# A listed instruction order for the opening of a fused attention and leaky-ReLU kernel, with separate places for four chunks

## The chip, the cores and the metric

The kernel runs on one core of one Trainium2 chip. A core has engines that run at the same time, each with a queue of its own that it works off strictly in order: TensorE (PE, matrix products, with a separate row PEld for the loading of the stationary operand), VectorE (DVE), ScalarE (ACT), GpSimd (POOL) and SyncE (SP), which here only issues DMA transfers. Engines wait for each other through semaphores. PE writes its results to PSUM; ACT and DVE read them from there; POOL and the DMA engines work on SBUF. The metric is the device time of one execution in microseconds (us), and lower is better.

## What is computed

The first part is a decayed linear attention over blocks of 64 tokens, the second a two-layer product with a leaky ReLU between.

```python
intra = np.einsum('bhic,bhjc->bhij', qb, kb) * Dmask[None]
intra = np.einsum('bhij,bhjd->bhid', intra, vb)
inter = np.einsum('bhid,bhde->bhie', qb * lam_pow[None], kv_state)
out[:, :, sl] = intra + inter
kb_dec = kb * rev_pow[None]
kv_state = lam_block * kv_state + np.einsum('bhsd,bhse->bhde', kb_dec, vb)
...
h = x @ w_in                       # x: 3072 x 512, w_in: 512 x 2048, float64
g = np.maximum(0.01 * h, h)
return (g @ w_out).astype(np.float32)   # w_out: 2048 x 512, float64
```

q, k and v are float32 of shape 4 x 8 x 768 x 64; the weights come as float64, and the output is float32.

## The kernel before

**Tiles.** The 3072 tokens are 24 chunks of 128 (two blocks of 64), six to a batch entry. Four chunks make a group of 512 tokens; there are six groups. w_in is cut into eight parts `p` of 256 columns.

**One chunk c.** SP loads k and q (two DMAs of 128 KB each) and v (one of 256 KB). PE transposes k and q (L406, L407), ACT copies the transposes out of PSUM (L414, L415). POOL or DVE scales k in place (L419), DVE or POOL scales the transposed q (L423). PE forms the scores (`go`, L433) and the state products (`kv`, L439); both go to the PSUM tile `psc`, scores in its lower half and states in its upper. DVE multiplies the scores by the decay (L452) and adds the state products to the running state (L457, L459), which POOL scales (L462). PE then forms the chunk's output in `po` (`own`, L472, and the two `inter` parts, L480), with a small copy of two columns between them (L491). ACT and DVE split the output into three float32r parts xh, xl, xm (L507, L508, L510).

**One weight part p.** A float64 half (512 KB) lands in one of three `raw` buffers. ACT makes three pieces of it (L578, L580, L582), DVE shifts and adds them to a float32 (L584, L585); with both halves done, the part is split into wh (ACT or DVE, L591 or L593), wl (DVE, L596) and wm (DVE, L602).

**up(g, p)** multiplies group g by part p: xh·wh and xl·wl for two blocks of 128 columns, an ACT rescale (L658), xm·wm, and the leaky ReLU on ACT (L661), then a store of 512 KB to DRAM (L664). A product of the full group is four matmuls of 512 columns. All `up` of groups 0 and 1 interleave with chunks 4 to 12; groups 2 to 5 follow. After that, `down` (L688) reads the stored results back and multiplies them by w_out; it fills the second part of the time.

**What sets the order.** Every step is an operation added to `Plan` with an engine (or two to choose from), an estimated length and the names it reads and writes; dependencies follow from the names. `emit` (L83) places operations greedily by estimated start time and rank, with PE operations of one round of a chunk locked together (`chains`), sorts them by that time and issues them: each engine's queue has that order for good. A second pass (L146 to L159) re-estimates times, and where PE would idle over 0.4 us it puts in unused 128 x 128 transposes (`busy`, L263) as long as the bank `b10` is not in use. Eleven such transposes run at the start (L268).

**Places.** Chunk c uses place `c % 2` of k, q, v and their transposes (`of`, L326), so chunk c + 2 can't be loaded before chunk c has been used. Scores and states share the one name `psc`: the DVE reads of either wait for both, and both products of the next chunk wait for all those reads.

**The end.** After `emit`, 32 matmuls whose results nothing uses are issued (L793 to L809): 24 with 512 columns on strips of the array, and 8 with 64 columns, which the trace records as 16.

Of the kernel before, what the change touches and what calls it, by code (L numbers as in the profile page):

```python
# [34 lines left out]


class Plan:

# [6 lines left out]
    def __init__(self):  # L45
        self.ops, self.last, self.rank = [], {}, 0.0
        self.chain, self.chains = None, {}
        self.warm, self.slack, self.more = 0.0, 0.0, {}
        self.first = {"PE": 0.0, "ACT": 0.0, "DVE": 3.4, "POOL": 0.0, "DMA": 0.2}
        self.cold, self.idle, self.spare = 6.0, None, None  # L50

    def begin(self, name):
# [30 lines left out]
    def emit(self):  # L83
        n = len(self.ops)
        follows, heads = {}, {}
        for c in self.chains.values():
            m = [i for i in c if "PE" in self.ops[i][0]]
            for i in c[1:]:
                self.ops[m[0]][2].update(self.ops[i][2] - set(c))
            heads[m[0]] = m[1:]  # L90
            follows.update((i, m[0]) for i in m[1:])
# [21 lines left out]
        done = []  # L113
        while len(done) < n:
            best = None
            for e in free:
                for i in able[e]:
                    if e == "PE" and (i != locked[0] if locked else i in follows):
                        continue
                    t = max(free[e], since(i, e))  # L120
                    if (best is None or (t, self.ops[i][3]) < best[:2]) and good(i, e, t):
                        best = (t, self.ops[i][3], i, e)
            t, _, i, e = best
            ways, fn = self.ops[i][:2]
            if i in heads:
                locked = list(heads[i])
            elif locked and i == locked[0]:
                locked.pop(0)
            for x in ways:
# [8 lines left out]
            for u in users[i]:  # L138
                ends[u].append((free[e] + self.more.get(i, 0.0), e))
                left[u] -= 1  # L140
                if not left[u]:
                    for x in self.ops[u][0]:
                        able[x].add(u)
        self.timeline = sorted(done)

# [3 lines left out]
        for t, _, i, e in self.timeline:  # L149
            ways, fn, deps = self.ops[i][:3]  # L150
            t = max([soon[e]] + [over[d][0] + (0.0 if over[d][1] == e != "DMA" else self.SOON[over[d][1]]) for d in deps])
            if e == "PE":
                if self.spare in self.ops[i][4]:
                    self.idle = None
                if self.idle is not None and t > soon[e] + 0.4:
                    self.idle(int((t - soon[e] - 0.2) / 0.22))
# [6 lines left out]
def kernel(  # L163
# [32 lines left out]
    GOFIRST = 3  # L196
    SUBL, FIRST = 0.75, -8.0

    DV = 10
# [22 lines left out]

    W = [[sb([P, 4 * 2 * P], f"w{x}{p}", F32R) for x in "hlm"] for p in range(NP)]
    X = [[sb([P, KO, T], f"x{x}{i}", F32R) for x in "hlm"] for i in range(2)]
# [22 lines left out]
    kqv = [[x[:, i * H * D:(i + 1) * H * D].rearrange("p (h d) -> p h d", h=H) for i in range(2)] for x in kqv_f]  # L247
    kTs, qTs, qsTs = ([part(HP * C).rearrange("p (y t) -> p y t", y=HP) for _ in range(2)] for _ in range(3))
    sc = part(2 * HP * C2).rearrange("p (x y t) -> p x y t", x=2, y=HP)
    state = [part(HP * D).rearrange("p (y d) -> p y d", y=HP) for _ in range(4)]  # L250
# [56 lines left out]
    add("DVE", 1.95, factors_k, [], ["fk", "sc"])  # L307
    add("DVE", 1.25, factors_q, [], ["fq"])
    ENG = {"ACT": nc.scalar, "DVE": nc.vector, "POOL": nc.gpsimd}
# [16 lines left out]
    def of(c):  # L326
        return c // NCB, c % NCB, c % 2

# [98 lines left out]
    def scores(c):  # L427
# [17 lines left out]
        if c < GOFIRST:  # L445
            add("PE", 0.47, go, [f"kT{i}", f"qT{i}"], ["psc"])
        add("PE", 0.47, kv, [f"k{i}", f"v{i}"], ["psc"])
        if c >= GOFIRST:
            add("PE", 0.47, go, [f"kT{i}", f"qT{i}"], ["psc"])

        def uses():
            add("DVE", 0.69, lambda: nc.vector.tensor_tensor(sc, psc[:, :, lower, :], decay, op=ALU.mult), ["psc", "fk"], ["sc"])  # L452
            for t in range(n_pu):
                j = 2 * c + t
                new = state[j % 4]
                if n == 0 and t == 0:
                    add("DVE", 0.42, lambda new=new: nc.vector.tensor_copy(new, pu[0]), ["psc"], [f"st{j % 4}"])  # L457
                else:
                    add("DVE", 0.42, lambda new=new, t=t: nc.vector.tensor_tensor(new, new, pu[t], op=ALU.add),  # L459
                        ["psc"], [f"st{j % 4}"])  # L460
                if n_pu == 2:
                    add("POOL", 0.7, lambda new=new, j=j: nc.gpsimd.tensor_tensor(state[(j + 1) % 4], new, _bc(lam_c, 2, D), op=ALU.mult),  # L462
                        [f"st{j % 4}", "fq"], [f"st{(j + 1) % 4}"])
# [123 lines left out]
    def parts(p, src, keys):  # L587
        wh, wl, wm = W[p]
        def head(e):
            if e == "ACT":  # L590
                nc.scalar.activation(out=wh, in_=src, func=AF.Copy, bias=0.0, scale=NEAR / S)  # L591
            else:
                nc.vector.tensor_scalar(wh, src, NEAR / S, None, op0=ALU.mult)  # L593

        add(("ACT", "DVE"), (1.05, 0.7), head, keys, [f"wh{p}"])
        add("DVE", 1.25, lambda: nc.vector.scalar_tensor_tensor(wl, wh.bitcast(F32), -S, src, op0=ALU.mult, op1=ALU.add),  # L596
            keys + [f"wh{p}"], [f"wl{p}"])
        difference(p)

    def difference(p):  # L600
        wh, wl, wm = W[p]
        add("DVE", 1.25, lambda: nc.vector.scalar_tensor_tensor(wm, wl.bitcast(F32), 1.0, wh.bitcast(F32), op0=ALU.mult, op1=ALU.subtract),  # L602
            [f"wh{p}", f"wl{p}"], [f"wm{p}"])

    def w_in(p):
        for h in range(2):
            to_float32("wi", p, h, w32[:, h, :], f"w32{h}")
        parts(p, w32f, ["w320", "w321"])

# [153 lines left out]
    for n, x in enumerate(seq):  # L763
# [15 lines left out]
        elif x[0] == "wp":  # L779
            if not freed:  # L780
                add("DVE", 0.0, lambda: None, [], ATT + [f"gr{j}" for j in range(NR)])
                add("ACT", 0.0, lambda: None, [], [f"raw{j}" for j in range(NRAW)] + ["t0", "t1"])
# [5 lines left out]
        else:  # L788
            down(*x[1:])
    plan.emit()  # L790


    a, b = ring[0][0], W[0][0]  # L793
    spare = acc[0] + acc[1]

    def strips(n, times):

        k = P // n
        for _ in range(times):
            for i in range(n):  # L800
                r = slice(i * k, (i + 1) * k)
                nc.tensor.matmul(spare[i], lhsT=a[r, 0:P], rhs=b[r, 0:T], start=True, stop=True, skip_group_check=True)  # L802

    strips(2, 6)
    strips(4, 3)
    f = graw[0]
    for _ in range(4):
        for i in range(2):
            nc.tensor.matmul(spare[2][HALF[i], 0:C2], lhsT=f[:, 0:C2], rhs=f[:, 0:C2], start=True, stop=True, skip_group_check=True)  # L809

# [29 lines left out]
```

## Time and profile before

The time is 611.25 us, the median of three runs (610.77 to 612.51). The profiled execution has a span of 610.29 us from its first to its last instruction.

| what | us |
|---|---|
| median of the runs | 611.25 |
| span of the profiled execution | 610.29 |
| PE busy | 601.9 |
| DVE busy | 313.2 |
| ACT busy | 269.9 |
| POOL busy | 86.6 |
| first product with a weight part (`up(0, 1)`) starts | 30.41 |
| last product of `down` starts to end | 605.17 to 606.28 |
| last unused product ends | 609.39 |

"Busy" counts an engine's instructions and leaves out its waits. PE's matmuls overlap in a pipeline, so that a busy PE may still run below its peak; the start-to-start distance of two matmuls is the better price: 0.227 us for 512 columns in the stream that fills most of the span. A wait is given as the idle time ahead of an instruction with what ended it.

### The profile page before, as it was taken

To read this page: it belongs to the slowest core of one execution; us is meant where nothing else is said; L and a number is where in the kernel's file an instruction comes from. 1 tells how busy PE (TensorE), PEld (TensorE's weight loads), DVE (VectorE), ACT (ScalarE), POOL (GpSimd) and SP (SyncE) were. 2 spreads that over 40 slices of the span, in tenths; PEclk is the share of its full clock that TensorE was granted. 3 is DMA by queue.
4 is the path that set the end of the run, shared out by engine and by line. 5 is a ranking of instruction groups with operands and counts; after the bars stand their busy time and mean duration, and the time that the engine had idled before them with its cause. 6 is when DMAs were issued, how large, how long until landed. Compare 5 with 4: busy or idle time off the path is not lost.

```text
span 610.3 us, 13012 instructions
## 1 busy us (share of the span) xinstructions
PE 601.9 (99%) x5426; PEld 497.6 (82%) x5426; DVE 313.2 (51%) x418; ACT 269.9 (44%) x430; POOL 86.6 (14%) x90
## 2 busy tenths in 40 slices
PE   7799999999999999999999999999999999999999
PEld 5688888888888878888788888888888888888887
DVE  5899764334243426326366755545454544636531
ACT  4678974444455646555577522222222313214111
POOL 2564412114133004104000000000000000000000
PEclk9899999999999999999999999999999999999999
DMA  9999775666889878886686843524333343333201
GB/s 201 236 261 263 215 204 126 175 154 176 192 212 245 212 222 219 212 242 212 233 302 219 278 155 103 173 69 139 137 104 134 111 136 111 132 104 126 82 1 69
DMA packets 147754, 105.18 MB, mean 172 GB/s; under 512 B 123632, under 2 KB 124400, under 8 KB 147696
## 3 DMA queue, kind: packets, MB, share of 16 engines
q1 hardware_dynamic: 147552, 104.36, 58.8%
q8 instruction: 42, 0.69, 0.5%
q14 instruction: 16, 0.13, 0.1%
q10 hardware_dynamic: 144, 0.00, 0.0%
HBM read 68.69 MB, written 35.65 MB: 171 GB/s over the span
## 4 chain that ended last, share of the span: by engine, by line
PE 95%; DMA 2%; ACT 1%; DVE 1%; issue 0%; SPq 0%; ACTq 0%
PE b L640 42%; PE b L700 18%; PE po L700 11%; PE psc L700 11%; PE po L313 4%; PE psc L313 4%; PE pt L700 4%; DMA g<-gs 1%; DMA att<-in_v_dram 1%; PE pt L403 1%; DMA att<-in_q_dram 1%; PE po L403 0%; PE psc L802 0%; ACT att L415 0%; PE b L266 0%
## 5 line engine op out<-in xcount | busy, mean ns | idle before, releaser
L682 ACT ACTIVATE xh<-att 128x1024 fp32r<-128x1024 f32 x48 | 50.8, 1060 | 149.1 <-PE b L700 133.6
L683 DVE SCALAR_TENSOR_TENSOR xl<-att,xh 128x1024 fp32r<-128x1024 f32 x48 | 58.7, 1223 | 97.5 <-ACT xh L682 97.5
L640 PE MATMUL b<-xm,wm 128*128 128x512 f32 (+2 forms) x392 | 104.5, 392 | 0.7 <-ACT b L658 0.7
L640 PE MATMUL b<-xh,wh 128*128 128x512 f32 (+2 forms) x392 | 103.2, 386 | 0.8 <-ACT xh L507 0.8
L640 PE MATMUL b<-xl,wl 128*128 128x512 f32 (+2 forms) x392 | 103.4, 387 | 0.0
L640 PEld LDWEIGHTS b<-xh,wh 128*128 128x128 f32 x392 | 72.9, 188 | 16.0 <-ACT xh L507 0.9
L640 PEld LDWEIGHTS b<-xl,wl 128*128 128x128 f32 x392 | 72.7, 188 | 15.1 <-DVE wl L596 0.3
L640 PEld LDWEIGHTS b<-xm,wm 128*128 128x128 f32 x392 | 71.4, 188 | 16.0 <-ACT b L658 1.1
L658 ACT ACTIVATE b<-b 128x512 f32<-128x512 f32 (+2 forms) x97 | 56.1, 580 | 60.6 <-PE b L640 60.5
L661 ACT ACTIVATE gs<-b 128x512 f32<-128x512 f32 (+2 forms) x97 | 57.0, 592 | 44.2 <-PE b L640 38.3
L700 PE MATMUL b<-wh,xh 128*128 128x512 f32 x192 | 74.7, 389 | 0.0
L700 PE MATMUL b<-wl,xl 128*128 128x512 f32 x192 | 74.7, 389 | 0.0
L685 DVE SCALAR_TENSOR_TENSOR xm<-xl,xh 128x1024 fp32r<-128x1024 f32 x48 | 58.7, 1225 | 4.7
L462 POOL TENSOR_TENSOR att<-att 128x256 f32<-128x256 f32 x40 | 34.4, 861 | 58.7 <-DVE att L459 58.7
L700 PEld LDWEIGHTS b<-wh,xh 128*128 128x128 f32 x192 | 36.1, 188 | 7.5
L700 PEld LDWEIGHTS b<-wl,xl 128*128 128x128 f32 x192 | 36.0, 188 | 7.5
L423 POOL TENSOR_TENSOR att<-att 128x512 f32<-128x512 f32 (+1 forms) x20 | 25.3, 1265 | 95.6 <-PE po L313 34.7
L452 DVE TENSOR_TENSOR att<-psc,att 128x512 f32<-128x512 f32 x24 | 16.5, 689 | 43.1 <-PE psc L313 43.1
L584 DVE TENSOR_SCALAR w<-w 128x512 int32<-128x512 int32 x32 | 19.6, 612 | 36.0 <-ACT w L578 35.9
L700 PE MATMUL psc<-wh,xh 128*128 128x512 f32 x96 | 37.3, 389 | 0.0
L700 PE MATMUL psc<-wl,xl 128*128 128x512 f32 x96 | 37.3, 389 | 0.0
L700 PE MATMUL psc<-wm,xm 128*128 128x512 f32 x96 | 37.3, 389 | 0.0
(79 smaller groups left out, 810.4 us busy)
## 6 DMA issues: line engine op xcount, KB each, us to landing
att<-g SPq DMA_DIRECT2D x48, 512.0 KB, 3.3
g<-gs SPq DMA_DIRECT2D x47, 512.0 KB, 4.0
raw<-in_moe_w_in_dram SPq DMA_DIRECT2D x16, 512.0 KB, 5.5
raw<-in_moe_w_out_dram SPq DMA_DIRECT2D x16, 512.0 KB, 4.8
att<-in_k_dram SPq DMA_DIRECT2D x48, 128.0 KB, 4.3
att<-in_v_dram SPq DMA_DIRECT2D x24, 256.0 KB, 4.5
out_dram<-gs SPq DMA_DIRECT2D x23, 256.0 KB, 2.1
wo<-w SPq DMA_DIRECT2D x8, 512.0 KB, 5.9
```

Source lines behind the costliest of these rows:

```text
L313: nc.tensor.matmul(dst[HALF[cols]], lhsT=lhsT[HALF[rows]], rhs=rhs[HALF[rows]], start=start, stop=True, skip_group_check=True)
L423: add(eng, us, lambda: e.tensor_tensor(o, x, _bc(pow_q, 2, 2)[:, :, m, :], op=ALU.mult), ["fq", dep], [f"qsT{i}"])
L452: add("DVE", 0.69, lambda: nc.vector.tensor_tensor(sc, psc[:, :, lower, :], decay, op=ALU.mult), ["psc", "fk"], ["sc"])
L462: add("POOL", 0.7, lambda new=new, j=j: nc.gpsimd.tensor_tensor(state[(j + 1) % 4], new, _bc(lam_c, 2, D), op=ALU.mult), [f"st{j % 4}", "f ...
L584: add("DVE", 0.42, lambda: nc.vector.tensor_scalar(d, d, 3, None, op0=ALU.logical_shift_left), [], [key])
L640: nc.tensor.matmul(dst, lhsT=w[z][:, kk * 2 * P + f * P:kk * 2 * P + (f + 1) * P], rhs=x[z][:, kk, toks], start=start and kk == 0, stop=kk ...
L658: add("ACT", ns, lambda b=b: nc.scalar.activation(out=b, in_=b, func=AF.Copy, bias=0.0, scale=S + 1.0), [], [kb], rank=-1.5)
L661: add("ACT", ns, lambda b=b, r=r: nc.scalar.activation(out=r, in_=b, func=AF.Prelu, bias=0.0, scale=1.0 / WS, alpha=0.01), [kb], [f"gs{jg} ...
L682: add("ACT", 1.05, lambda: nc.scalar.activation(out=h, in_=graw[j], func=AF.Copy, bias=0.0, scale=NEAR), reads, wr("h"))
L683: add("DVE", 1.25, lambda: nc.vector.scalar_tensor_tensor(l, graw[j], 1.0, h.bitcast(F32), op0=ALU.mult, op1=ALU.subtract), reads + [f"rh{ ...
L685: add("DVE", 1.25, lambda: nc.vector.scalar_tensor_tensor(m, l.bitcast(F32), -S, h.bitcast(F32), op0=ALU.mult, op1=ALU.add), [f"rh{j}", f" ...
L700: nc.tensor.matmul(acc[tb][z // 2][:, cols], lhsT=ring[j][z][:, f * T + tb * P:f * T + (tb + 1) * P], rhs=W[pp][z][:, f * d_model:(f + 1) ...
```

## The change

**A listed order.** `ORDER` lists operations 0 to 710 of the plan, which are all of groups 0 and 1, by number; a letter behind a number names the engine where two are possible (a = ACT, v = DVE, p = POOL), and `f6` asks for six unused transposes before the next PE operation. `emit` places these first, in this order, without ranks and without the locked rounds, and goes on greedily behind them. The automatic filling of PE gaps is off; only the listed fillings remain (6, 5, 4 and 3). The queues open as follows (T = transpose, SC = scores, KV = state products, OWN and I0, I1 = output parts, the digit is the chunk):

```
PE after:  f6 Tk0 Tq0 f5 KV0 Tq1 Tk1 SC0 Tk2 OWN0 I0 SC1 I1 Tq2 KV1 f4 OWN1 SC2 I0 I1 KV2 Tk3 Tq3
           OWN2 I0 SC3 I1 KV3 f3 OWN3 I0 I1 Tq4 up(0,1): h h l l, Tk4, m m, up(0,0): h h l l, Tq5 SC4 KV4 ...
SP after:  q0 k0 q1 v0 k1 k2 q2 v2 v1 raw(1) k3 q3 raw(1) v3 q4 raw(0) raw(0) k4 raw(2) q5 raw(2) v4 ...
SP before: k0 q0 v0 k1 q1 v1 raw(1) q2 k2 raw(1) v2 q3 k3 q4 v3 raw(0) k4 q5 v4 raw(0) k5 q6 v5 ...
```

In the DVE queue, the scaling of k of chunk 0 is gone (now POOL's first operation); the copies L491 of chunks 3, 4, 5 and 7 are on DVE; wh of parts 2, 3, 5 and 6 has moved to ACT, wh of parts 4 and 7 to DVE.

**Places.** Chunks 2, 3, 4 and 5 get places of their own in the memory of weight parts 5, 6, 7 and 4, which are written late; a zero-length operation keeps each part from being written before its chunk is done. Chunks 6 and on use the two old places.

**Names.** `psc` is split into `psS` (scores) and `psK` (states).

**The end.** The unused products behind `emit` are gone.

```diff
+        for i, e in self.listed:
+            e = e or next(iter(self.ops[i][0]))
+            assert i in able[e]
+            put(i, e, max(free[e], since(i, e)))
...
-                if self.spare in self.ops[i][4]:
+                if self.spare in self.ops[i][4] and not self.listed:
                     self.idle = None
-                if self.idle is not None and t > soon[e] + 0.4:
+                if i in self.fill:
+                    self.idle(self.fill[i])
+                elif not self.listed and self.idle is not None and t > soon[e] + 0.4:
...
+    OWN = {2: 5, 3: 6, 4: 7, 5: 4}
...
+    for p in OWN.values():
+        for j, (x, y) in enumerate(zip(kqv, (kTs, qTs, qsTs))):
+            z = W[p][j]
+            x.append(z[:, :H * D].rearrange("p (h d) -> p h d", h=H))
+            y.append(z[:, H * D:].rearrange("p (y t) -> p y t", y=HP))
...
-        return c // NCB, c % NCB, c % 2
+        return c // NCB, c % NCB, c % 2 if c not in OWN else 2 + list(OWN).index(c)
...
-            add("PE", 0.47, go, [f"kT{i}", f"qT{i}"], ["psc"])
-        add("PE", 0.47, kv, [f"k{i}", f"v{i}"], ["psc"])
+            add("PE", 0.47, go, [f"kT{i}", f"qT{i}"], ["psS"])
+        add("PE", 0.47, kv, [f"k{i}", f"v{i}"], ["psK"])
...
-            add("DVE", 0.69, lambda: nc.vector.tensor_tensor(sc, psc[:, :, lower, :], decay, op=ALU.mult), ["psc", "fk"], ["sc"])
+            add("DVE", 0.69, lambda: nc.vector.tensor_tensor(sc, psc[:, :, lower, :], decay, op=ALU.mult), ["psS", "fk"], ["sc"])
...
+        if p in OWN.values():
+            i = 2 + list(OWN.values()).index(p)
+            add("DVE", 0.0, lambda: W[p].__setitem__(slice(3), weights(p)), [],
+                [f"{x}{i}" for x in ("k", "q", "v", "kT", "qT", "qsT")] + [f"w{x}{p}" for x in "hlm"])
...
-    strips(2, 6)
-    strips(4, 3)
-    f = graw[0]
-    for _ in range(4):
-        for i in range(2):
-            nc.tensor.matmul(spare[2][HALF[i], 0:C2], lhsT=f[:, 0:C2], rhs=f[:, 0:C2], start=True, stop=True, skip_group_check=True)
```

## The prediction

> **What bounds the kernel now.** I read the page's busy shares and slices first, then the table by stages, then the rows of PE, DVE and SP around the first 40 us, and last the end of the span.
>
> ```profile
> PE 601.9 (99%) x5426; PEld 497.6 (82%) x5426; DVE 313.2 (51%) x418; ACT 269.9 (44%) x430; POOL 86.6 (14%) x90
> ...
> PE   7799999999999999999999999999999999999999
> ...
> DVE  5899764334243426326366755545454544636531
> ...
> PE 95%; DMA 2%; ACT 1%; DVE 1%; issue 0%; SPq 0%; ACTq 0%
> ```
>
> PE is the bound, but its first two slices (15 us each) are not full, and DVE is fullest in slices 2 to 4. The table by stages has, for each stretch, the busy time of PE, PEld, DVE, ACT and POOL, then the granted clock, the share of the DMA engines and GB/s:
>
> ```profile
> 4.00:15.00 11.00, 9.10 (x208) 6.75 (x209) 7.62 (x24) 5.33 (x10) 2.26 (x3) 1.00 1.13 236
> 15.00:25.00 10.00, 7.51 (x248) 5.72 (x251) 8.51 (x14) 6.96 (x13) 6.83 (x7) 1.00 1.02 244
> 25.00:30.40 5.40, 4.62 (x115) 3.80 (x104) 4.35 (x6) 2.70 (x6) 1.49 (x3) 0.69 0.91 228
> 30.40:38.20 7.80, 7.79 (x96) 6.45 (x97) 7.56 (x11) 5.53 (x10) 4.91 (x4) 1.00 1.01 284
> 38.20:55.60 17.40, 17.40 (x305) 14.55 (x305) 16.34 (x23) 15.42 (x29) 8.36 (x7) 1.00 0.90 251
> 100.00:606.20 506.20, 505.24 (x3863) 417.84 (x3861) 233.40 (x291) 198.98 (x307) 43.80 (x48) 1.00 0.55 163
> ```
>
> From 30.4 us on PE has no gap worth a name. So what this change can win lies before 30.4, and in the end. The timeline shows how the opening is lost:
>
> ```profile
> 24.43 1.57 PE L313 MATMUL psc<-att 64*64 64x64 f32 x64 [1.79 <-DMA att<-in_v_dram]
> ...
> 30.41 2.12 PE L640 MATMUL b<-xh,wh 128*128 128x512 f32 x8 [0.78 <-ACT xh L507]
> ```
>
> The scores of chunk 3 wait for its v, which SP issues at 19.07 and which lands at 24.30. Before 30.41 PE does 10 transposes of a tile at 0.44 (start-to-start at 59.27 and 59.70) and four chunks' scores, states and outputs at 2.03 (51.66 to 53.69): 4.4 + 8.1 = 12.5 us. From the first transpose at 4.04 that leaves 30.41 - 4.04 - 12.5 = **13.9 us lost** to waits, unused transposes and half clock. The clock is at half in one stretch of 3.4 us (25.0 to 28.4; 0.69 in the third row). It costs 0.64 on scores and states (1.57 against 0.93), 0.53 on outputs (1.39 against 0.86) and 0.14 on a transpose, 1.3 us together.
>
> DVE is the second bound. In the opening its rows swell whenever POOL works:
>
> ```profile
> 15.90 1.22 DVE L584 TENSOR_SCALAR w<-w 128x512 int32<-128x512 int32 x1
> ```
>
> **The change, part by part.**
>
> *The end.* The last unused product starts at 608.70 and takes 0.69, to 609.39:
>
> ```profile
> 608.70 0.69 PE L809 MATMUL po<-att 128*64 128x64 f32 x16
> ```
>
> The last output transfer is issued at 607.3 and lands 1.7 later, at 609.0. SP waits for both before it closes, so the removal saves 609.39 - 609.0 = **0.4 us**, and no more, since the transfer is next. If that transfer took 0.4 longer, nothing.
>
> *Places and load order.* SP's first 14 entries wait for no buffer now. Equal bytes should land at the times of before: 256 KB by 4.6, 1.28 MB by 9.4, 3.1 MB by 16.4. v of chunk 3 has 4.2 MB up to itself; the 3.1 MB at 16.4, and then 0.5 us for each 128 KB (its pace from 10.4 to 16.4) give 16.4 + 8 x 0.5 = 20.4, at most 21.4 at the pace that followed. So the wait at 24.43 goes, 3 to 4 us earlier. What is late next is DVE.
>
> *The DVE queue to the first product.* I sum the rows of before in the new order, each without its overlap with the row ahead, up to the first state addition of chunk 3: decay factors 3.15, four score products 2.76, seven state operations 2.31, four scalings of q 2.32, three xl 1.80, two xm 1.29, two shifts 1.90, one sum 0.60: 16.1 us from 3.44. Scaling k of chunk 0 (0.67) is on POOL now, beside its landing, where POOL is idle. To this come DVE's own waits. Before they are 5.8 (1.3, 1.9, 0.2, 0.2, 2.1). In the new order: 0.3 for the first transpose; 1.7 for states 0, since v0 lands at 8.2 and PE takes 0.6; 1.3 for scores 0, which PE does behind the transpose of k1, landed at 9.4; 1.0 for scores 1, behind the output of chunk 0. That is 4.3, so the state addition ends at 3.44 + 16.1 + 4.3 = 23.9. Behind it in the chain: an output part on PE 0.4, the sum at L585 (1.1, running since 23.9) and the small copy 0.15, the last output part 0.45, and on ACT wh of part 1 (1.06, behind that sum) and xh 0.5. **The first product starts at 26.7**, against 30.41. The floor that the DMA alone sets is 20.4 + 0.6 + 0.4 + 0.4 + 0.3 + 0.5 + 0.6 for the small waits = 23.2; I use 24.0 for a best case.
>
> *The next weight part.* PE then has up(0, 1), 6 x 0.907 = 5.44, and one transpose, 0.44: it asks for wh of part 0 at 32.6. DVE's sum up to there is 27.1, with 4.3 and another 0.4 of waits: 35.2. In this sum eight rows are slower than the same row with POOL idle (shifts 1.22, 0.84 and 0.84 against 0.43; sums 1.20 and 1.46 against 0.69; wl 1.64 against 1.22; xm 1.07 against 0.69; wh 1.43 against 0.69): 4.4 us of excess. The new order puts two of POOL's scalings into the first 12 us, where DVE waits anyway; without all the excess the 35.2 would be 30.8, under PE's own 32.6. Between 32.6 and 35.2 I take 33.4, nearer to the lower end because of those two. Before, this product started at 38.24, with KV4 and SC4 (0.93) and two more transposes (0.87) done ahead of it: 38.24 - 33.4 - 1.8 = **3.0 us gained** there, 1.2 and 3.8 at the two ends, 6.5 with the best case's 24.0 (24.0 + 5.9 = 29.9).
>
> *Later stalls.* From 38.2 to 55.6 DVE was idle for 17.40 - 16.34 = 1.06 us only, and its products came just in time (wl of part 2 ended at 47.75 and PE used it at 47.80). The new DVE queue holds entries that wait for PE: the scores of chunk 4, which PE now does behind four products of part 0 (2.3 us of DVE idle by the sums above), the small copies of chunks 4 and 5 (0.5 each), and the sum of part 3 behind ACT (1.9). Behind them in the queue stand wl and wm of parts 2 and 3, for which PE waits. That is 5.2 of idle time against 1.06: a cost of 0 where those parts are ready early anyway, up to 4.2 where none is. I take 0.6, near zero, because PE's queue also moved chunk work ahead of those parts.
>
> *Split names.* Scores may start while the states are still read. In the rows of before PE waited 1.1 and 0.5 us for a state addition ahead of scores; this is in the sums above and not counted again. Worth 0 to 1.6.
>
> *Fewer fillings.* 18 listed transposes against 19: at 0.11 to 0.24 us each no difference, unless the clock falls.
>
> *Sum.* 3.0 + 0.4 - 0.6 = 2.8 us. The span of 610.3 becomes **607.5**; the median of the runs is 0.96 above the profiled span, so 608.4 us.
>
> The price of a quiet opening needs one more row: the clock fell at 25.0 though PE's longest gap there was 1.79 us. By the section "Part 1: The HAM clock gate" of the Trainium skill's page "TensorE: Matmul & The Clock Gate", it falls after at least one idle window of about 3.4 us. By that rule no gap of the new opening would be long enough, and the half clock would be gone for good; this case's trace, with 1.79, doesn't agree, so the rival below keeps its chance.
>
> **The rivals.**
>
> 1. *The DVE wait is less than I think* and the half clock goes: the first product at 24.0, 6.5 + 0.4 and 0.6 to 1.4 of stalls: 605.5. For it: 4.4 us of excess that hangs on POOL's timing. Against: DVE's own waits at the start, which the landings fix. Chance 0.12.
> 2. *The stall only moves* to wh of part 0 at 35.2: 1.2 + 0.4 - 0.8 = 0.8 gained, 610.4. For it: DVE busy 97% in 30.4 to 38.2. Against: POOL's earlier start. Chance 0.23.
> 3. *The half clock comes back in the stream of products*, where every matmul pays: 3.4 us at half cost 1.7, so 610.1. For it: from 5.8 to 26.7 PE has only 12.5 us of work and 2 of fillings, 30% idle. Against: fillings stand in the longest gaps. Chance 0.10.
> 4. *Slower: the fixed DVE queue starves PE.* The 5.2 us of DVE idle behind chunk 4 is uncovered: 1.2 + 0.4 - 4.2 = -2.6, 613.8. It decides once DVE is idle for over 2.7 us between 38 and 56, the 1.06 of before and the 1.6 gained. For it: 47.75 against 47.80. Against: the DVE queue arrives there ahead of the old one. Chance 0.10.
>
> That the change doesn't do what it says is possible only for the names: if the waits stay joint, 0 to 1.6 is missing, which rivals 2 and 4 cover.
>
> **How the numbers follow.** The forecast, 608.4, has chance 0.45, with its own range 606.6 to 610.2 (the 1.2 to 3.8 of the weight part, and stalls). Low: rival 1 reaches to 605.4. High: rivals 2 and 3 lie inside 611.6, rival 4 outside. I count a difference over 0.3%, 1.8 us, as more than the measurement's scatter: faster below 609.4, slower above 613.1. Faster: most of the forecast (0.38), rival 1 (0.12) and the near edges of rivals 2 and 3 (0.06): 0.56. Slower: rival 4 and the far edge of rival 3: 0.12. The same: 0.32.
>
> **What would show it.** In the profile of the changed kernel: no wait for v of chunk 3; the first L640 row near 26.7; a wait of about 0.8 us for wh ahead of part 0 near 33; DVE idle in 38 to 56 of 1 to 3 us; no L802 and L809 rows and the last transfer's landing as the end. Wrong would be a first product later than 29, or gaps of PE over 3 us in sum after 35, or a second stretch at half clock.

## The result, and the profile after

The changed kernel takes 620.31 us, the median of four runs (619.05 to 620.9), against 611.26 us for the kernel before beside it (610.77 to 612.51). The ratio is 1.014, with a 95% interval of 1.012 to 1.0159: 9 us slower, where 608.4 was forecast.

The page's busy line of PE and the two lines of its chain that ended last, changed kernel:

```profile
PE 600.1 (97%) x5385; PEld 495.1 (80%) x5385; DVE 308.5 (50%) x419; ACT 266.3 (43%) x428; POOL 85.1 (14%) x91
...
PE 84%; SPq 7%; DMA 6%; ACT 1%; issue 1%; DVE 0%; POOL 0%; DVEq 0%; ACTq 0%
PE b L698 34%; PE b L758 18%; PE po L758 11%; PE psc L758 11%; SPq L427 4%; PE pt L758 4%; PE po L366 3%; PE psc L366 3%; DMA att<-in_v_dram 3%; SPq L391 2%; DMA wo<-w 1%; DMA raw<-in_moe_w_in_dram 1%; DMA g<-gs 1%; SPq L441 0%; ACT gs L719 0%
```

PE is not busier but idler: 17.2 us of the span without a matmul, against 8.4. SP's queue, at 0% of the chain before, now has 7% of it, and over half of that is one line: L427 (L374 before), the small loads of quarter heads of k and q that DVE transposes for chunks 10 and on. (Lines have moved: the `up` products L640 to L698, the leaky ReLU L661 to L719, its store L664 to L722, v L388 to L441, scores and states L313 to L366.)

To see where the time went I add up PE's work in the order of the matmuls' starts, leave the fillings out, count a matmul at its undisturbed price (0.227 us for 512 columns, 0.108 for 128 columns of a transpose, 0.0156 for 64 columns), and compare when two kernels reach the same sum. Difference to the kernel before, in us (positive is later), at the times of the kernel before:

```
at us                    24    40    52    60    75    95   115   130   145   160   300
changed kernel          1.6  -1.0  -1.0   0.2   0.8   0.8   2.4   6.7   7.8   7.8   7.4
order_of_before         0.3  -0.3   0.1   0.1   0.5   0.5   0.5   0.5   0.5   0.5  -0.9
opening_of_list_54      0.2  -2.7  -2.6   1.4   1.1   1.1   1.1   1.1   1.1   1.1  -0.4
few_small_changed       1.4   0.2   0.2   1.3   1.7   2.9   3.7   4.0   3.9   3.9   2.9
small_loads_on_pool     2.9  -0.1   0.0   1.1   1.8   3.1   3.8   5.8   5.7   5.7   4.7
sp_planned_late         2.1  -0.8  -0.8   0.3   0.6   0.5   1.3   9.9   9.8   9.8   9.3
batch15_behind          2.7   0.3   0.3   1.4   1.7   1.6   3.1   7.5   7.5   7.5   9.6
no_list                 0.8   1.2   4.7   7.0   6.5   6.5   6.5   6.0   7.5   7.5   7.9
```

The first row is the result in short. In this execution the opening wins 1 us at 40 to 52 us. Then 8.7 us are lost between 52 and 145 us, most of them behind 95, in a stretch in which the kernel before has no gap. (The other rows are the experiments.) Each row is one profiled execution, and in the first 60 us two executions of the same opening differ by up to 2 us (at 40 us the run few_small_before is some 2 us behind the kernel before, and its opening is the same). So the rows are to be read by what they do behind 60, and the 1 us won is no more than that scatter.

PE's rows with a wait between 96 and 146 us, and the table by stages (busy PE, PEld, DVE, ACT, POOL, then clock, DMA share, GB/s), both of the changed kernel:

```profile
97.24 1.20 PE L698 MATMUL b<-xh,wh 128*128 128x512 f32 x4 [0.49 <-ACT gs L719]
121.79 0.62 PE L366 MATMUL psc<-att 64*64 64x64 f32 x14 [1.25 <-DMA att<-in_v_dram]
125.49 2.11 PE L698 MATMUL b<-xh,wh 128*128 128x512 f32 x8 [0.74 <-ACT gs L719]
132.19 0.69 PE L366 MATMUL psc<-att 64*64 64x64 f32 x32 [1.23 <-DMA att<-in_v_dram]
145.46 1.21 PE L698 MATMUL b<-xh,wh 128*128 128x512 f32 x4 [0.91 <-ACT gs L719]
```

```profile
97.00:120.00 23.00, 22.76 (x268) 18.12 (x272) 12.55 (x19) 8.87 (x17) 5.38 (x6) 1.00 0.72 165
120.00:145.00 25.00, 21.33 (x271) 16.30 (x260) 11.35 (x27) 7.60 (x14) 6.42 (x7) 1.00 0.79 185
```

The same stages before:

```profile
97.00:120.00 23.00, 23.00 (x221) 19.08 (x220) 5.65 (x10) 10.76 (x19) 3.36 (x3) 1.00 0.60 156
120.00:145.00 25.00, 25.00 (x332) 20.70 (x331) 9.88 (x22) 10.29 (x19) 6.18 (x8) 1.00 0.70 168
```

Two things are waited for in turn: v of a chunk, and a leaky ReLU (L719) that can't write `gs` until the last store has read it. Both are SP's (the ReLU itself waited for stores for 4.7 us between 60 and 160 us). The five gaps make 4.6 us. From 60 to 160 us PE's weight loads also wait for this ReLU, 4.3 us in all; in the kernel before they wait for no other engine there. In these two stages DVE is busy for 55% of the time at most, and ACT for 39%. SP's own waits between 75 and 155 us (line <- what it waited for: us, times, longest), first of the changed kernel, then of the kernel before:

```profile
SPq L722 <- ACT gs L719: 2.2, 1, 2.2
SPq L427 <- DMA raw<-in_moe_w_in_dram: 1.4, 1, 1.4
SPq L619 <- ACT low L635: 0.8, 1, 0.8
```

```profile
SPq L664 <- ACT gs L661: 14.0, 10, 2.9
SPq L388 <- PE po L313: 7.6, 4, 2.5
SPq L338 <- PE b L640: 1.8, 2, 1.3
```

This is the view that decides. Before, SP stood ready for ten of the stores before their data were: a store left the moment the ReLU ended. In all it waited 25.3 of these 80 us, and 6.0 after; from 95 to 155 us alone the same view gives 19.3 before and 2.0 after. Counted from its timeline:

| SP, 75 to 155 us | before | after |
|---|---|---|
| small loads | 71 | 95 |
| median time to issue one | 0.47 | 0.47 |
| all issues | 103 | 127 |
| time spent issuing, us | 53.4 | 68.3 |

(Some rows of single loads, up to 1.46 us, hold a wait as well, so the last line is an upper bound.) Over the 80 us the 68.3 us would still fit. They don't fit in the stretch in which the list asks for them. The chain of work that ended last, followed back from 150 to 100 us, first of the changed kernel, then of the kernel before, has SP's small loads as its second largest part after, and PE alone before:

```profile
by line: PE b L698 37.2%; SPq L427 33.7%; DMA att<-in_v_dram 6.9%; DMA g<-gs 6.3%; issue 4.8%; SPq L391 3.5%; ACT gs L719 2.4%; PE psc L366 2.2%; ACT b L716 1.2%; SPq L441 0.9%; SPq L722 0.9%; PE po L366 0.5%; ACTq L719 0.1%
```

```profile
by line: PE b L640 84.8%; PE po L313 8.7%; PE psc L313 7.3%
```

The DMA engines behind the queue are no slower: from 75 to 155 us the median time from issue to landing is 2.4 us for a small load in both kernels, 3.7 against 3.9 before for a v, and 2.9 against 3.0 for a store. What is late is the issue.

SP's timeline of the changed kernel at 118 to 128 us shows what stands around a store (L722) and v (L441):

```profile
118.19 0.50 SPq L441 DMA_DIRECT2D att<-in_v_dram  x1
118.74 1.08 SPq L427 DMA_DIRECT2D raw<-in_k_dram  x2
119.92 0.41 SPq L722 DMA_DIRECT2D g<-gs  x1
120.38 0.44 SPq L427 DMA_DIRECT2D low<-in_q_dram  x1
120.86 2.93 SPq L427 DMA_DIRECT2D raw<-in_k_dram  x4
...
125.48 1.50 SPq L427 DMA_DIRECT2D raw<-in_k_dram  x3
127.08 0.41 SPq L722 DMA_DIRECT2D g<-gs  x1
127.59 0.39 SPq L441 DMA_DIRECT2D att<-in_v_dram  x1
```

In these rows a store of 512 KB takes SP 0.41 us and a small load of 48 KB 0.47: SP pays by the issue, not by the byte. The Trainium skill's page "Perfetto Trace Analysis", section "DMA Instruction — HWDGE (DVE, Sync)", says that the sequencer is held while the descriptors are generated and that the data movement isn't in its profiled time. These rows agree with the second, since a store that SP issues in 0.41 us lands 2.9 us after its issue (median); no row here shows the descriptors.

### The profile page after: what moved, and what is told of

Its sections match the earlier page's. It is cut to its first block, busy times and chain, and to the rows that moved or that the text cites. A ratio compares the mean times of both kernels' runs of the same rounds, so it can differ in the third digit from the quotient of the medians.

```text
span 617.3 us, 12905 instructions
## 1 busy us (share of the span) xinstructions
PE 600.1 (97%) x5385; PEld 495.1 (80%) x5385; DVE 308.5 (50%) x419; ACT 266.3 (43%) x428; POOL 85.1 (14%) x91
## 4 chain that ended last, share of the span: by engine, by line
PE 84%; SPq 7%; DMA 6%; ACT 1%; issue 1%; DVE 0%; POOL 0%; DVEq 0%; ACTq 0%
PE b L698 34%; PE b L758 18%; PE po L758 11%; PE psc L758 11%; SPq L427 4%; PE pt L758 4%; PE po L366 3%; PE psc L366 3%; DMA att<-in_v_dram 3%; SPq L391 2%; DMA wo<-w 1%; DMA raw<-in_moe_w_in_dram 1%; DMA g<-gs 1%; SPq L441 0%; ACT gs L719 0%
## 5 line engine op out<-in xcount | busy, mean ns | idle before, releaser
L698 PE MATMUL b<-xh,wh 128*128 128x512 f32 (+2 forms) x392 | 104.0, 391 | 2.3 <-ACT gs L719 2.1
L698 PE MATMUL b<-xm,wm 128*128 128x512 f32 (+2 forms) x392 | 103.5, 393 | 0.3 <-ACT b L716 0.3
L698 PE MATMUL b<-xl,wl 128*128 128x512 f32 (+2 forms) x392 | 102.0, 386 | 0.0
L698 PEld LDWEIGHTS b<-xh,wh 128*128 128x128 f32 x392 | 71.8, 188 | 19.4 <-ACT gs L719 4.6
L698 PEld LDWEIGHTS b<-xl,wl 128*128 128x128 f32 x392 | 73.0, 188 | 14.9
L698 PEld LDWEIGHTS b<-xm,wm 128*128 128x128 f32 x392 | 70.7, 188 | 16.6 <-ACT b L716 2.5
L719 ACT ACTIVATE gs<-b 128x512 f32<-128x512 f32 (+1 forms) x97 | 56.9, 592 | 49.7 <-PE b L698 40.1
L515 POOL TENSOR_TENSOR att<-att 128x256 f32<-128x256 f32 x40 | 32.5, 813 | 105.5 <-DVE att L512 97.3
L512 DVE TENSOR_TENSOR att<-att,psc 128x256 f32<-128x256 f32 x40 | 16.6, 415 | 57.2 <-PE psc L366 52.9
L637 DVE TENSOR_SCALAR w<-w 128x512 int32<-128x512 int32 x32 | 17.4, 558 | 46.1 <-ACT w L631 46.1
L758 PE MATMUL po<-wh,xh 128*128 128x512 f32 x96 | 37.3, 389 | 0.0
```

Of the source, the lines that this page charges most:

```text
L637: add("DVE", 0.42, lambda: nc.vector.tensor_scalar(d, d, 3, None, op0=ALU.logical_shift_left), [], [key])
L698: nc.tensor.matmul(dst, lhsT=w[z][:, kk * 2 * P + f * P:kk * 2 * P + (f + 1) * P], rhs=x[z][:, kk, toks], start=start and kk == 0, stop=kk ...
L719: add("ACT", ns, lambda b=b, r=r: nc.scalar.activation(out=r, in_=b, func=AF.Prelu, bias=0.0, scale=1.0 / WS, alpha=0.01), [kb], [f"gs{jg} ...
L758: nc.tensor.matmul(acc[tb][z // 2][:, cols], lhsT=ring[j][z][:, f * T + tb * P:f * T + (tb + 1) * P], rhs=W[pp][z][:, f * d_model:(f + 1) ...
```

## The experiments

Ratios are to the kernel before, measured beside each run.

**Three quarters of the small loads gone.** In both kernels, four small loads of each pair of heads become one whole load of as many bytes, in batches 10, 12 and 15 (a batch bears the number of its first chunk); chunks 10 to 17 then get wrong rows of k and q.

```diff
...
+                        if c < 18:
+                            o = sub[:, y - lo, :].rearrange("p (h d) -> p h d", d=D)
+                            z = src[b, 0:o.shape[1], n * C:(n + 1) * C, :].rearrange("h p d -> p h d")
+                            go = lambda o=o, z=z, a=a: a or nc.sync.dma_start(out=o, in_=z)
...
```

> The changed kernel, with the 32 small k and q loads of each of the batches of chunks 10 to 11, 12 to 14 and 15 to 17 (96 loads, each of one quarter of one pair of heads) replaced by 8 whole loads a batch (24 in all) of as many bytes in the place of the first of every four; every other entry of every queue stays where it is. The attention of chunks 10 to 17 so gets the wrong rows of k and q. Theory A (SP's own queue is the bound from 75 to 155 us: at some 0.5 us for each small load it hands out v loads and stores of the products late): 72 issues of 0.5 us, 36 us of SP's time, go, and TensorE's waits for v and for the relu between 95 and 150 us go with them: 613 to 615 us, 5 to 7 below the changed kernel's 620.3. Theory B (the listed order of ScalarE and VectorE is what holds the products up, SP only follows): within 1 us of 620.3. Theory C (the score and state products that are waited for apart disturb each other in the shared bank): within 1 us of 620.3.

> The kernel before with the same 96 small loads replaced by 24 whole ones (the attention of chunks 10 to 17 gets the wrong rows). Its SP often idled until the next store was ready, so theory A expects little: 609 to 611.3 us against 611.3. Were it to fall by 5 us or more, SP's time would be a bound in both kernels, and it would not explain what the change lost.

Measured: the changed kernel 612.75 us (1.0017, 1.0001 to 1.0032), the kernel before 611.99 (1.0002, 0.9988 to 1.0017). With the list, 72 issues fewer are worth 7.6 us; without it, nothing. Every other entry of every queue, PE's order too, stays, so theories B and C fall as the main cause. SP's waits of the changed kernel without these loads, 75 to 155 us:

```profile
SPq L728 <- ACT gs L725: 23.4, 8, 5.0
SPq L391 <- PE psc L366: 6.1, 1, 6.1
SPq L447 <- PE po L366: 3.2, 2, 2.9
```

SP waits for the ReLU again, as before. But the profiled execution (614.54 us, 1.8 above the median of its kernel) still loses 3.7 us between 52 and 145 us (table above), so a smaller part need not be SP's. There PE's weight loads wait for ACT, 2.9 us for the rescale and 1.5 for the ReLU between 60 and 160 us, and for DVE not at all.

**SP's entries placed by the planner behind the 44th.** Ahead of each listed operation it puts the transfers that the operation needs, then those that can start by its time.

```diff
...
+            if e == "DMA":
+                n_dma += 1
+                if n_dma <= 44:
+                    at.add(i)
+                    put(i, e, max(free[e], since(i, e)))
+                continue
...
```

> The changed kernel with its listed order kept for all four computing engines to the end of the list, and for SP only for its first 44 entries; after these the planner's own rule (earliest possible start, then due time) places SP's entries among the listed operations, as it does in the kernel before. Theory A: stores and v loads come ahead of small loads by up to 17 places, and 4 to 7 us come back: 613.5 to 616.5. Theory B and C: within 1 us of 620.3, since the computing engines' orders are those of the list.

Measured: 621.3 us (1.0154, 1.0134 to 1.0174). A miss for theory A as I had put it; by its number the run is where theories B and C had it. Until 115 us the trace is 1 us better than the changed kernel; then, with v and stores ahead, the small loads are what comes late:

```profile
127.42 0.46 PE L394 MATMUL psc<-att 64*64 64x64 f32 x16 [1.39 <-DVE att L464]
...
133.38 0.92 PE L394 MATMUL psc<-att 64*64 64x64 f32 x24 [2.58 <-DMA att<-in_v_dram]
```

(L464 is DVE's transpose of the small loads here.) Behind these two waits PE also runs at half clock from 131.0 to 137.9 us of its trace, which costs up to 3.4 of the 8.6 us that the table shows lost between 115 and 130. So this other order within SP's queue doesn't help: it moves the wait from one load to another. That no order would, this run doesn't show.

**The list emptied.** `ORDER` has no entries; places, names and the missing end products stay.

> The changed kernel with an empty list: places of their own for chunks 2 to 5, the two names for scores and states, and no unused products at the end, all in the planner's own order. Theories A and B (the list makes the loss): 608 to 612 us, that is near the 611.3 of the kernel before. Theory C: 618 or more, since the two names are still there. If what lies outside the profiled span stays near 1.8 us (it was 0.97 before), the removed products at the end make that part.

Measured: 619.62 us (1.0128, 1.0098 to 1.0159). Against theories A and B, and for C by its number, yet not by its place: this kernel loses 7 us before 60 us and little behind (table above), the changed kernel the other way round. With the new places and names free to use, the greedy planner chooses another order, and that one loses in the opening. Which of the two freedoms misleads it was not tested.

**The same places, in the order of before.** The list is replaced by the order that the planner had made for the kernel before, with its fillings:

```diff
-3 2 26 0 4 25 1 f6 5 6 48 9p 8 10 7 49 f5 12 50 29 14 28 ...
+2 3 4 0 25 26 1 5 27 7 9 6 94 8 10 f3 11 49 f3 12 28 13 48 ...
```

> The changed kernel with another list: the order, engine by engine, that the planner had worked out for the kernel before, with its fillings, up to 175 us. So places of their own, two names and no products at the end, but not one instruction moved. Theory A3 (all of the loss is in the order, and the places and names cost nothing of themselves): 610 to 612. If the places or the names cost time (two names in one bank, or places whose W tile has to be claimed): 614 or more.

Measured: 611.23 us (1.0, 0.999 to 1.001). This settles the parts: own places, split names and the missing end products together cost or win no more than 0.6 us. All of the 9 us is in the order.

**The end products alone.** The kernel before without L793 to L809.

> The kernel before without the matrix products behind its last output, whose results nobody reads; nothing else differs. Theory D (these products cost nothing in the count of the device's time and their removal lengthens what lies outside the span): outside the span 1.7 to 1.8 us instead of 0.97, the span some 0.4 shorter, the median 0.3 to 0.8 us above the kernel before. The prediction's step (the end comes 0.4 us earlier, nothing else): median 0.4 below.

Measured: 610.97 us against 611.65 (0.9992, 0.9981 to 1.0004). It agrees with the predicted 0.4 and can't be told from nothing. Theory D falls: in every timed execution of every kernel here, the one before among them, 1.74 to 1.86 us lie outside the span. The 0.96 of the prediction came from setting one execution's span against the median of others.

**The list cut short, the planner behind.** `for x in ORDER.split()[:187]`, and likewise 322 and 445 of 715 entries.

> The changed kernel with its list cut after 187 of 715 entries, where the planner's clock stands at 45 us; the planner's own rule orders the rest. Theory A2 (the loss is made by what the list puts from 75 us on, and by nothing in the opening): with the opening's gain of 1 us at 45 us and the planner's order behind it, 609.5 to 612.5. Theory E (any order with these places and names loses behind the opening, as the kernel with the empty list lost 6 us before 65 us): 615 or more.

> As the run before, cut after 322 entries (planner's clock 74 us). Theory A2: 610 to 613, since the changed kernel is level with the one before at 70 us of its trace and adds 0.8 us outside its span. Theory E: 615 or more.

> As the run before, cut after 445 entries (planner's clock 101 us), which leaves the loads of the batch of chunks 12 to 14 and all later ones to the planner. Theory A2 with the loss spread over 75 to 145 us as SP's queue fills: 613 to 617. If the loss were made by the entries up to 101 us alone: 619 to 621. If by those behind alone: 611 to 613.

Measured: 617.13 (1.0094, 1.0058 to 1.0131), 617.81 (1.0103, 1.0082 to 1.0124) and 617.05 us (1.0092, 1.0071 to 1.0114). They are about 3 us better than the whole list, and all three the same. Theory A2 is missed: by 4 to 5 us in the first two, narrowly in the third. The first two lie where theory E had them, yet E as it stands falls with the run order_of_before, which has these places and names and loses nothing. The three runs don't locate the loss: the greedy planner can bring losses of its own behind each cut, as with the empty list.

**v of chunk 1 asked for earlier.**

```diff
-... 8 10 7 49 f5 12 50 29 14 28 11 27 30 ...
+... 8 10 7 27 49 f5 12 50 29 14 28 11 30 ...
```

> The changed kernel with one entry of its list moved: SP asks for v of chunk 1 two places earlier, ahead of q and v of chunk 2. In the changed kernel v of chunk 1 lands at 15.51, the state products of chunk 1 wait 1.93 us for it, and every profiled run of this list so far shows a granted clock of 0.5 to 0.8 at 16 to 24 us. Theory F (the fixed order asks for v of chunk 1 too late; the gap brings the half clock back and both make 2 to 3 us of the loss): v lands near 12.5, no gap, no half clock at 16 to 24, 617 to 618.5. If the half clock has another cause: 620 to 621.

Measured: 617.63 us (1.011, 1.0089 to 1.0131), 2.7 less than the changed kernel and within what theory F expected; the two intervals overlap, so the gain is likely and not shown. The wait for this v is gone. But the half clock is not, in the profiled execution (16.7 to 23.5 us, and once more from 122.5 to 125.9). The stages of this run:

```profile
12.00:16.00 4.00, 2.82 (x102) 2.30 (x92) 1.78 (x5) 1.72 (x4) 1.75 (x3) 1.00 1.18 273
16.00:20.00 4.00, 3.12 (x92) 2.70 (x94) 2.92 (x6) 2.13 (x4) 0.62 (x1) 0.59 0.93 222
20.00:24.00 4.00, 4.00 (x100) 3.55 (x100) 2.48 (x6) 1.94 (x4) 2.69 (x3) 0.56 1.15 309
```

So F is half right at most: the number fits, and the late v is not all that halves the clock.

**The opening of the list, then the order of before.** The list with v of chunk 1 earlier up to 187, 232 or 293 entries (45, 54, 68 us), behind it the order of before; one more with fillings (`f4 41` to `f8 41`, and `f4` ahead of 80).

> The list's own order up to its 187th entry (45 us), with v of chunk 1 two places earlier, and from there the order of the kernel before to 175 us. Theory A3 with F: the opening's gain of 1 us and the end's 0.4 to 0.7 are kept, nothing is lost behind: 608.5 to 611. If the order of before does not fit the state in which the list's opening leaves the engines: 613 or more.

> As the run before, with the list kept up to its 232nd entry (54 us). The changed kernel's trace is 0.95 us ahead of the one before at 52 us and level at 56. Theory A3 with F: 609 to 612. If the loss began with the entries at 45 to 54 us: 613 or more.

> The list kept up to its 293rd entry (68 us), v of chunk 1 two places earlier, the order of the kernel before behind it. The trace of the list cut at 54 us was 2.6 us ahead of the kernel before at 52 us and lost it in a wait of 1.81 us for VectorE at the seam and a half clock behind it. Theory G: nothing is lost behind 75 us; with the seam where the list's own order has passed its wait at 55 us: 609 to 611.5. If VectorE's total work up to 75 us takes the opening's gain back wherever the seam is: 611.5 to 613.

> As the run before, with four more fillings ahead of the products of scores and v of chunk 1 (the gap at 16.5 us) and four ahead of the state products of chunk 3 (the gap of 0.9 us at 24 us). Theory F2 (the half clock of 16 to 24 us comes with these gaps): granted clock 1.00 throughout, median 0.5 to 1.5 us below the run before. If fillings in a gap do nothing for the clock: the same, or up to 0.3 us more.

Measured: 612.79 (1.003, 1.0016 to 1.0045), 612.21 (1.0021, 1.0004 to 1.0038), 620.01 (1.0142, 1.0113 to 1.0171) and 620.94 us (1.0154, 1.013 to 1.0179). The first two keep nothing of the opening and lose 1 to 1.6 us; 612.79 and 612.21 lie between what A3 expected (up to 611 and 612) and its rival (613 or more). Their openings are the best of all, and the trace of the second says where it goes:

```profile
27.35 2.11 PE L701 MATMUL b<-xh,wh 128*128 128x512 f32 x8
33.41 2.10 PE L701 MATMUL b<-xh,wh 128*128 128x512 f32 x8
...
55.27 2.56 PE L701 MATMUL b<-xh,wh 128*128 128x512 f32 x8 [1.81 <-DVE wh L650]
```

The two first rows are up(0, 1) and up(0, 0), 3.1 and 4.8 us earlier than before (1.8 of the latter is work that came ahead of it there). At 52 us it is 2.6 us ahead; then one wait for wh, at the seam of the two orders, and a half clock behind it (0.82 at 58 to 64 us) take 4 us. The seam at 68 us fits worse: 9 to 11 us are lost at 60 to 78 us, with PE waiting for q and for ScalarE's rescale, and 6.8 us at half clock in each run, from 70.6 us on in the first (in two pieces) and from 74.5 in the second. The first misses both of its ranges, and neither says anything about VectorE. The fillings left the granted clock of 16 to 20 us at 0.57. That speaks against F2, but doesn't refute it: the longest gap there, 1.24 us up to 15.88, had none of the fillings in it.

**One batch of small loads taken out of the stretch.** 31 of the 32 entries of batch 15 leave the list; the planner places them behind it.

> The changed kernel with 31 entries taken out of its list: the small loads of the batch of chunks 15 to 17 (all but the first), which the planner then places behind the listed entries. All other entries stay in their order, and no work is left out. Theory G (the list asks three batches of small loads of SP within 70 us of TensorE's work, where the order of before takes 94 us for them, and SP, at 0.5 us a load, can't issue them in that time; this is the loss): 31 x 0.5 = 15.5 us of SP's time leave the stretch 130 to 155 us, the part of the loss that arises behind 128 us (3 us) comes back: 616.5 to 618. If SP's order only follows late computing engines: 620 to 621.

Measured: 621.15 us (1.0164, 1.0129 to 1.0199), no gain. The table by stages, first with batch 15 behind, then the changed kernel (second number: PE busy):

```profile
128.00:165.00 37.00, 36.09 (x378) 28.80 (x377) 12.59 (x28) 14.65 (x26) 9.75 (x10) 1.00 0.60 164
165.00:200.00 35.00, 34.40 (x505) 28.11 (x504) 14.90 (x28) 19.48 (x35) 9.29 (x10) 1.00 0.82 212
200.00:265.00 65.00, 63.57 (x720) 52.04 (x718) 24.54 (x46) 35.52 (x64) 12.99 (x15) 1.00 0.83 216
```

```profile
128.00:165.00 37.00, 34.86 (x371) 27.57 (x370) 12.89 (x29) 14.66 (x26) 9.81 (x10) 1.00 0.80 200
165.00:200.00 35.00, 35.00 (x511) 29.01 (x510) 15.52 (x27) 19.80 (x35) 9.11 (x10) 1.00 0.63 188
200.00:265.00 65.00, 64.67 (x726) 53.31 (x725) 24.92 (x45) 36.02 (x64) 13.73 (x16) 1.00 0.82 212
```

Of the expected 3 us, 1.2 us of idle PE come back at 128 to 165 us, and 1.7 us are lost at 165 to 265, where the loads now are. By its number the run fits the rival, that SP's order only follows late engines; by the trace it shows a loss that moves with the loads. Theory G's price for them was too high.

**A second queue for the small loads.** The 48 loads of q of the three batches are issued by GpSimd.

```diff
...
-                        move(0.55, lambda o=o, z=z: nc.sync.dma_start(
+                        move(0.55, lambda o=o, z=z, e=nc.sync if c >= 18 or nm == "k" else nc.gpsimd: e.dma_start(
...
```

> The changed kernel with its list as it is, and the 48 small loads of q of the batches of chunks 10 to 17 asked for by GpSimd's queue in place of SP's. No work is left out and no order changes. Theory G: half of the 96 small loads leave SP, 24 us of its time between 75 and 155 us, and most of the 6 to 7 us lost there comes back, less what GpSimd's own waits cost: 613 to 617. If SP's time is no bound: 620 or more. If an issue on GpSimd holds its products for k and the states up: above 621.

Measured: 616.11 us (1.0072, 1.0047 to 1.0096). All work is done, the list is the same, and 4.2 us come back; SP waits 31.6 of the 80 us again. The DMA engines are about as busy as in the changed kernel, 75.5% against 77.3% from 75 to 155 us. This is the cleanest evidence for theory G's core, that SP's issuing time binds the list. 4.5 us of the loss against the kernel before remain; in this run GpSimd, which also works for the states, issues loads for 29.9 us between 75 and 155, and what that costs was not separated.

**One load earlier in the order of before.** v of chunk 3 (entry 73) ahead of q of chunk 4 (110), possible only with its own place.

> The order of the kernel before, in the changed kernel's places (as in the run order_of_before), with one entry moved: SP asks for v of chunk 3 ahead of q of chunk 4. In the order of before these two loads of q stand ahead of it, 1.1 us of SP's time, and the state products of chunk 3 wait 1.5 to 1.8 us for v, which lands at 24.3. Theory H (an own place is worth what it lets SP ask for earlier, and the rest of before's order has room for it): the wait falls to 0.5 us or less, and about 1 us stays to the end, with the 0.3 to 0.7 us of the left-out products: 609.3 to 610.6. If VectorE, 95% busy at 28 to 64 us in the kernel before, takes it back: 610.8 to 611.6.

Measured: 612.33 us (1.0002, 0.9987 to 1.0017), against 612.08 for the kernel before beside it, so nothing is won and neither range is met. Its timeline:

```profile
23.84 0.85 PE L459 MATMUL pt<-att,wl 128*128 128x128 f32 x4 [1.45 <-DMA wl<-in_q_dram]
```

The wait for v is gone; the q behind it, which SP now asks for later, is waited for in its place, at the same time and for nearly as long. At 20 to 24 us the DMA engines are 92% busy; here moving one load ahead of another only changes the name of the wait. (VectorE is 100% busy from 16 to 24 us, so a part of it may be VectorE's.)

## Why the prediction was wrong

The step that failed is the sentence on the bound: "From 30.4 us on PE has no gap worth a name. So what this change can win lies before 30.4, and in the end." It is true of what can be won, and I let it stand for what can be lost. *Later stalls* then went on to 55.6 us, and for DVE alone. The list orders SP too, through all of groups 0 and 1, and I costed only its first 14 entries. That SP had 25.3 of 80 us to spare behind 75 us, and no more than that, was to be read in the profile of before: the view of SP's waits. The list puts the attention rounds 9 to 11 earlier among the `up` products: in the traces the outputs of chunks 9, 10 and 11 start 8.2, 8.1 and 14.9 us of PE's work earlier than before. So SP has 95 small loads to issue from 75 to 155 us in place of 71, with almost no wait left from 95 on. PE waits for what stands behind them, v and the stores, and 8.7 us are lost between 52 and 145 us. Taking 72 issues away gives 7.6 us back, and moving 48 of them to GpSimd 4.2.

Step by step:

- *The end*, 0.4: agrees with 0.7 in the median, not told from nothing.
- *v of chunk 3*, 20.4 to 21.4: landed at 21.73, 0.3 past the range, and nothing waited for it. Right in what it says of the wait.
- *The first product at 26.7*: 29.03 in the profile, past my own mark of 29. The timeline of the opening, changed kernel:

```profile
15.64 0.69 PE L366 MATMUL psc<-att 64*64 64x64 f32 x32 [1.93 <-DMA att<-in_v_dram]
...
25.18 1.05 PE L366 MATMUL psc<-wm,wh 64*64 64x64 f32 x32 [0.86 <-POOL att L515]
...
29.03 2.11 PE L698 MATMUL b<-xh,wh 128*128 128x512 f32 x8
35.10 2.09 PE L698 MATMUL b<-xh,wh 128*128 128x512 f32 x8
```

  My DVE waits had no entry for v of chunk 1, which the list asks for ninth (it landed at 15.51), and none for the half clock (0.75 and 0.83 at 16 to 24 us). Rival 3 had the half clock, in the wrong place. With that v two places earlier and the clock full, the run opening_of_list_54 started up(0, 1) at 27.35.
- *wh of part 0 taken at 33.4*, against 38.24: 35.10, and 33.41 in that run. That the second agrees with the prediction is luck. The step was a wait of 0.8 us for wh behind a product that ends at 32.6; in both runs PE came to this product with no wait, 6.07 and 6.06 us after up(0, 1), and only up(0, 1) was late. So DVE wasn't the bound here. Where the clock stays up, in the runs opening_of_list_45 and opening_of_list_54, the opening is 2.5 to 2.7 us ahead at 40 us. In the other 11 of the 13 profiled executions that begin with this list the clock falls to half between 15.5 and 18.4 us.
- *Later stalls*: DVE was idle for 6.0 us at 38.2 to 55.6 (11.37 busy of 17.40), more than my 5.2, and PE lost 0.5. Rival 4 named this as what decides; it doesn't. It had the sign, for a reason that the trace refutes, and of its 4.2 us only the 0.5 are there.
- *Split names*: nothing in the order of before, together with the places (order_of_before).
- *Sums*: two slips, which decide nothing. 3.44 + 16.1 + 4.3 is 23.8 and not 23.9, and the low end 606.6 doesn't follow from 3.8 + 0.4 us won, which give 607.0.

The sum of 2.8 us won was 1 at 52 us; the 8.7 lost behind it had no term.

What stays open: what halves the clock at 16 to 24 us; and what makes the 3.7 us that the list loses at 52 to 145 us without three quarters of the small loads, for which the waits of PE's weight loads name ACT, but no run tested it. A mended list that beats both kernels wasn't found; the lowest time, 610.97, is that of the kernel before without its end products, and it can't be told from the kernel before.

## What to carry to other kernels

When an order is fixed by hand, cost every queue it fixes to its end, the one that only issues DMAs first: count its issues, multiply by its own row, and compare with how long it waits now. Do it stretch by stretch, between one product that needs a transfer and the next. An average hides it: here 24 more issues, 14.9 us, would have fitted into the 25.3 us of waits over the 80 us, and yet the queue ran late. A queue that is idle a third of the time may be punctual only because of that. And a stage in which the bounding engine has no gap is one where a reordering of the other queues can hardly win, and can lose.

## What the runs showed of the hardware

- An issue costs SP about as much for 48 KB as for 512 KB: medians of 0.47 us for a small load, and of 0.41 (changed kernel) and 0.34 (before) for a store. On GpSimd a small load took 0.61 (run small_loads_on_pool).
- The granted clock isn't settled by the longest gap. v1_earlier and opening_of_list_54 have the same entries up to 54 us, gaps of at most 0.92 us at 12 to 20 us and PE busy 2.82 and 2.77 us of the 4 at 12 to 16; the first ran 16 to 24 us at 0.56 to 0.59, the second at 1.00. The empty list, with 2.69 of 4 busy at 20 to 24 us, kept 1.00 too.
